# A new order for the first batch of an attention and MLP kernel, and a second weight matrix loaded by rows

## The chip, the cores and the metric

The kernel runs on one core of a Trainium2 chip. The metric is the device time of one execution in microseconds. Before the change the median of three runs is 582.38 us (581.66 to 583.03).

## The reference

Eight batches of 448 tokens, 12 heads of 64 columns. Queries and keys are normalised by rows, attention is computed without a mask, and the result passes a layer norm and an MLP of 768 to 3072 to 768 columns with a residual.

```python
q_n, k_n = (rmsnorm(q, g_q), rmsnorm(k, g_k))
scores = scale * np.matmul(q_n, k_n.transpose(0, 1, 3, 2))
attn = np.exp(scores - np.max(scores, axis=-1, keepdims=True))
attn = attn / (np.sum(attn, axis=-1, keepdims=True) + 1e-09)
x = np.matmul(attn, v)          # heads side by side: (8, 448, 768)
xn = (x - mu) / np.sqrt(var + 1e-06) * g_ln
out = x + np.maximum(xn @ w_ch1, 0.0) @ w_ch2
```

## The kernel before

Work is counted in pairs of heads (48 pairs, six a batch) and in units of one or two pairs, by which q, k and v are loaded and prepared. Batch 0 consists of units 0 to 3: unit 0 holds pair 0, unit 1 pair 1, unit 2 pairs 2 and 3, unit 3 pairs 4 and 5. From batch 1 on every unit has two pairs: unit 4 pairs 6 and 7, and so on. A pass over a unit of one pair has 448 columns, over one of two pairs 896.

All engines run their instructions in the order in which the program gives them out. For the first batch, and the preparation of some units of the second, this order is written out by hand in `ORDER` (L36), which `first_attention` (L490) walks through. The entries are:

- the preparation of unit u (`pieces`, L233). `a` and `c` square k and q (on ScalarE, or on GpSimd for those in `POOL_SQUARE`), `d` and `e` sum the squares (VectorE), `g` (or `gq` and `gk`) takes the inverse root on ScalarE, `i` multiplies k by the gains (GpSimd, or VectorE for units in `DVE_KG`), `j` makes k's high half in 16 bits (GpSimd for units in `POOL_HI`, else ScalarE), `k` the low half (GpSimd for `POOL_LO`, else VectorE), `l` scales q (VectorE), `m` copies it into a second half (GpSimd for `POOL_DUP`, else VectorE), and `z` casts v on GpSimd. `i0` also multiplies the two gains and spreads them over the partitions with a small matmul, `psG`.
- `Kp` and `Qp`: seven transposes on TensorE for pair p, and a copy out of PSUM (VectorE; for pairs in `ACT_Q` the copy of q is on ScalarE). The keys of all pairs go through the bank `tr`; the queries of batch 0 through a bank of the pool of three called `mlp`, those of pair 6 on through `tr`.
- `Sp.i` and `Vp.i`: piece i of 7 of the scores of pair p, with the exponential on ScalarE behind each (two banks in turn), and of the product with v; the last piece, `Vp.6`, is followed by two reciprocals and two multiplications on VectorE (`evac_o`, L464).
- `T`, `A`, `R`, `N`, `X`: the statistics of the layer norm, their joining, its root, the normalised tile and its transposes (`ln_trans`, L682: the first tile through `tr` with two copies on ScalarE, the second through an `mlp` bank, the third through `tr` with a copy on VectorE). `U0` to `U2` are the first three columns of tiles of the MLP (`up_first`, L937), one token tile each, with the activation behind `U2`. `M` takes a few minima and maxima for a check at the end.
- `L` loads a unit (SP's queue), `W` a third of W1 (GpSimd's queue), `G` and `G2` load and scale the norm's gain.
- `Hn` and `Jn`: n matmuls whose result nobody reads. `H` multiplies an identity by itself into the bank `psW`, `J` transposes an identity into `tr`. They lie in TensorE's queue like any other matmul.

Behind the list, `run_rest` (L976) goes through the batches. It takes the MLP of batch b in chunks (`mlp_chunks`), and between them gives out the steps of the attention of batch b+1 (`attention`, L540), spread evenly so that they end `TAIL[b]` chunks ahead of the batch's end; the layer norm of the next batch follows in these last chunks. Batch 0 has 21 chunks of the up projection (`up`, L713) and then 24 of the down projection (`down`, L723): for each of two column halves g and three token tiles t, four chunks of six of the 24 row tiles of W2. A bank of the pool `mlp` collects all 24, and `add` (L754) then adds it into x on VectorE, scaled.

From batch 1 on the down projection uses sums of blocks of W2 (a scheme with seven products in place of eight). With W2 in four blocks B11 to B22 (rows by columns), T1 = B12 - B11, T2 = B22 - T1, T3 = B12 - B22 (in place) and T4 = B21 - T2, each cut into four parts. `weight_sums` (L760) makes them on VectorE, one part behind each of certain chunks: eight parts, T1 and T2 in turn, in the last ten chunks of batch 0, then T3 and T4 in batch 1.

W2 is loaded by GpSimd's queue with a cast (`load_w2`, L611), at the steps `W2_AT` of the attention: its left column half as one transfer, later its right half as two.

Of the kernel before, what the change touches and what calls it, by code (L numbers as in the profile page):

```python
# [8 lines left out]
FP32 = mybir.dt.float32  # L9
# [7 lines left out]
ts = bass.ts  # L17
# [9 lines left out]
EXP_BIAS = -4.0  # L27
DVE_KG, POOL_HI, POOL_DUP, ACT_Q = (0, 6), (1, 2, 3, 4, 5, 6, *range(8, 25)), (3, 4, 5, 6), (0, 2, 4, 5)
POOL_SQUARE, POOL_LO = ((2, 1), (4, 0), (6, 0)), (5, 6)

# [61 lines left out]
class _Fast:  # L92
# [140 lines left out]
    def pieces(self, u):  # L233
# [4 lines left out]
        c = {}  # L238
# [86 lines left out]
        def qdup():  # L325
            (nc.gpsimd if u in POOL_DUP else nc.vector).tensor_copy(out=c["qn"][:, :, 1],
                                                            in_=c["qn"][:, :, 0])

# [34 lines left out]
    def trans_k(self, p):  # L363
        nc, sh = self.nc, self.sh
        u, w = PAIR_UNIT[p]
        qn, khl = self.units[u][0:2]
        kT, ps = self.kU[PE_SET][:, 960 * (p % 2):960 * (p % 2) + 960], self.tr
        nc.tensor.matmul(ps[:, 0:256].rearrange("p (e o) -> p e o", e=2)[:, :, 0:D],
                         khl[:, self.group(p, 6)], sh.id16, is_transpose=True, start=True, stop=False)
        for i in range(6):  # L370
            nc.tensor.matmul(ps[:, 192 + 128 * i:320 + 128 * i], khl[:, self.group(p, i)], sh.id16,
                             is_transpose=True, start=False, stop=(i == 5))
        nc.vector.tensor_copy(out=kT, in_=ps[:, 0:960])

# [236 lines left out]
    def load_w2(self, g):  # L611
        if g:
            self.nc.gpsimd.tensor_copy(out=self.rr[:, DMA_UNIT:DMA_UNIT + 1],
                                       in_=self.kU[DMA_UNIT % 2][:, 0:1])
        for c in (slice(0, HALF), slice(HALF, NFF)) if g else (slice(0, NFF),):
            self.nc.gpsimd.dma_start(
                out=self.sh.w2[:, c, ts(g, 384)],
                in_=self.w2[128 * c.start:128 * c.stop, ts(g, 384)].rearrange("(c p) d -> p c d", p=128))

# [88 lines left out]
    def first_mlp(self):  # L708
# [39 lines left out]

# [11 lines left out]
    def weight_sums(self):  # L760

        nc, w2, w2s = self.nc, self.sh.w2, self.w2s
        sub = lambda out, a, b: nc.vector.tensor_tensor(out=out, in0=a, in1=b, op=ALU.subtract)  # L763
# [212 lines left out]
    def run_rest(self):  # L976
        steps, mark, upto = self.steps, self.mark, self.upto
        for b in range(B):
# [19 lines left out]
            for cost, emit in chunks:  # L998
# [252 lines left out]
```

## Time and profile before

| | |
|---|---|
| median of three runs | 582.38 us |
| the profiled execution's own time | 579.58 us |
| its span in the trace | 578.0 us |
| TensorE busy | 559.5 us, 97% of the span |
| VectorE busy | 381.7 us, 66% |
| ScalarE busy | 364.4 us, 63% |
| GpSimd busy | 207.0 us, 36% |

The span runs from the first to the last instruction of the profiled execution; 1.58 us of its own time lie around it. Times in the timelines count from the span's start. A row of a timeline gives the start, the length, the engine (PE is TensorE, DVE VectorE, ACT ScalarE, POOL GpSimd), the line of the kernel, the operation, its tiles, and in brackets how long the engine had been idle and what it seems to have waited for. A matmul's length holds its way through the array, so that matmuls in a row overlap; how fast they follow each other is read from how much longer a longer row takes.

### The profile page before, as it was taken

Reading aid. Unit: us, or ns where it says so; the run is one execution under the profiler, and the core shown is the slowest. Engines: PE = TensorE matmul, PEld = TensorE weight load, DVE = VectorE, ACT = ScalarE, POOL = GpSimd, SP = SyncE. Lnnn points to the kernel's source line nnn. Section 1 sums busy time; section 2 is a strip of 40 time slices with the busy share of each in tenths; the row PEclk is TensorE's granted clock in tenths of the full one; section 3 lists DMA queues with packets and bytes.
Section 4 is the critical chain, followed back from the end, with each engine's and each line's share of the span. In section 5 each row is a group of like instructions: output and inputs, shape, how many; then the busy total and the mean of one; then the engine's idle time right before and its main releaser. Section 6 shows DMA issues by size and latency. Waiting matters only on the chain.

```text
span 578.0 us, 13670 instructions
## 1 busy us (share of the span) xinstructions
PE 559.5 (97%) x5446; PEld 411.9 (71%) x5446; DVE 381.7 (66%) x826; ACT 364.4 (63%) x674; POOL 207.0 (36%) x224
## 2 busy tenths in 40 slices
PE   5788999999999999999999999999999999999997
PEld 4556666687686867777677768777777777878684
DVE  6989567699657586845667586854756743664424
ACT  5998787447675779557775588637777477323130
POOL 5885636404440620654241521644242320020000
PEclk9999999999999999999999999999999999999999
DMA  8999999958672876969663798958743390030201
GB/s 206 251 238 222 214 207 165 193 147 137 124 131 77 158 127 145 127 148 121 121 106 48 184 134 136 128 143 122 145 64 65 119 113 1 1 110 1 83 2 58
DMA packets 178329, 72.59 MB, mean 126 GB/s; under 512 B 138212, under 2 KB 173220, under 8 KB 178260
## 3 DMA queue, kind: packets, MB, share of 16 engines
q1 hardware_dynamic: 133876, 52.52, 44.1%
q0 software_dynamic: 43440, 18.52, 25.2%
q8 instruction: 44, 0.72, 0.5%
q10 hardware_dynamic: 944, 0.62, 0.4%
q14 instruction: 25, 0.20, 0.1%
HBM read 52.76 MB, written 11.01 MB: 110 GB/s over the span
## 4 chain that ended last, share of the span: by engine, by line
PE 77%; DVE 1%; issue 0%; DVEq 0%
PE psH L798 33%; PE psP L821 30%; PE psS L405 7%; PE oA L458 4%; PE oB L460 1%; PE psS L411 1%; DVE qn L83 0%; DVE w2s L763 0%; DVE ssq L265 0%; DVE w L763 0%; DVE xn L662 0%; DVE hS L804 0%; DVE x L475 0%; DVE xl L757 0%; DVE xl L480 0%
## 5 line engine op out<-in xcount | busy, mean ns | idle before, releaser
L421 ACT ACTIVATE E<-psS,rr_all 128x448 f16<-128x448 f32 x336 | 204.6, 634 | 47.3 <-PE psS L405 40.3
L798 PE MATMUL psH<-xnT,w 128*128 128x256 f16 (+1 forms) x2016 | 225.7, 261 | 0.0
L798 PEld LDWEIGHTS <-w 128*128 128x128 f16 x2016 | 172.8, 98 | 24.3 <-issue 4.9
L801 ACT ACTIVATE hS<-psH 128x512 f16<-128x512 f32 x150 | 89.8, 599 | 97.2 <-PE psH L798 93.0
L821 PEld LDWEIGHTS <-hS 128*128 128x128 f16 x1080 | 100.0, 98 | 57.3 <-issue 1.1
L821 PE MATMUL psP<-w,hS 128*128 128x384 f16 x672 | 127.0, 326 | 0.0
L405 PE MATMUL psS<-qU,kU 128*128 128x448 f16 x288 | 100.9, 352 | 5.0 <-ACT E L421 3.2
L458 PEld LDWEIGHTS <-E 128*128 128x128 f16 x1008 | 70.3, 98 | 35.8 <-issue 2.8
L279 POOL TENSOR_TENSOR k<-k,gprod 128x896 f32<-128x896 f32 x18 | 38.9, 2160 | 139.5 <-ACT khl L259 113.2
L804 DVE TENSOR_TENSOR hS<-hS 128x512 f16<-128x512 f16 (+1 forms) x119 | 60.2, 512 | 19.3 <-ACT hS L801 17.8
L821 PE MATMUL psP<-w2s,hS 128*128 128x384 f16 (+1 forms) x408 | 69.9, 321 | 0.0
L458 PE MATMUL oA<-v,E 128*128 128x65 f16 x864 | 66.9, 193 | 1.1 <-ACT E L421 0.6
L757 DVE SCALAR_TENSOR_TENSOR x<-psP,rs_all,x 128x384 f32<-128x384 f32 x60 | 36.4, 617 | 42.4 <-PE psP L821 41.8
L460 PE MATMUL oB<-v,E 128*128 128x65 f16 x288 | 52.0, 193 | 0.1
L832 POOL TENSOR_TENSOR x<-x,hS 128x384 f32<-128x384 f32 x21 | 23.4, 1126 | 76.1 <-ACT hS L900 75.5
L473 DVE RECIPROCAL rec_all<-oA 128x6 f32<-128x6 f32 x48 | 9.2, 193 | 53.6 <-PE oA L458 53.5
L216 POOL DMA_DIRECT2D v<-in_v_dram x54 | 41.5, 781 | 4.0 <-PE oB L460 2.7
L405 PEld LDWEIGHTS <-kU 128*128 128x128 f16 x288 | 28.0, 98 | 11.1 <-issue 2.2
L900 ACT ACTIVATE hS<-hS,rs_all 128x384 f32<-128x384 f32 x27 | 14.6, 604 | 33.0 <-DVE hS L804 33.0
L460 PEld LDWEIGHTS <-E 128*128 128x128 f16 x336 | 32.4, 96 | 0.4 <-DVE xl L480 0.3
L83 DVE SCALAR_TENSOR_TENSOR qn<-q,rr_all 128x256 f16<-128x256 f32 (+2 forms) x69 | 24.8, 420 | 7.2 <-ACT rr_all L269 7.1
L265 DVE TENSOR_REDUCE ssq<-khl 128x14 f32<-128x896 f32 (+1 forms) x24 | 25.5, 1061 | 5.0 <-ACT khl L259 4.8
(145 smaller groups left out, 616.6 us busy)
## 6 DMA issues: line engine op xcount, KB each, us to landing
k<-in_k_dram SPq DMA_DIRECT2D x19, 384.0 KB, 4.2
q<-in_q_dram SPq DMA_DIRECT2D x18, 384.0 KB, 3.9
out_dram<-x SPq DMA_DIRECT2D x14, 384.0 KB, 3.0
w<-in_moe_w_ch_dram POOLq DMA_DIRECT2D x3, 1536.0 KB, 14.3
v<-in_v_dram POOLq DMA_DIRECT2D x54, 64.0 KB, 4.4
out_dram<-x POOLq DMA_DIRECT2D x9, 384.0 KB, 2.7
w<-in_moe_w_ch_dram POOLq DMA_DIRECT2D x1, 2304.0 KB, 22.5
w<-in_moe_w_ch_dram POOLq DMA_DIRECT2D x2, 1152.0 KB, 14.4
```

Source lines behind the costliest of these rows:

```text
L216: nc.gpsimd.dma_start(out[:, :, j, 0:D], main[:, :, j])
L265: nc.vector.tensor_reduce(out=c["ssq"][:, n], in_=c["sq", n], axis=AX.X, op=ALU.add)
L279: (nc.vector if u in DVE_KG else nc.gpsimd).tensor_tensor(out=c["t"][1], in0=c["t"][1], in1=sh.gprod.unsqueeze(1).broadcast_to([128, g, D] ...
L405: nc.tensor.matmul(ps[0][:, 0:S], c["main"][:, ts(i, 128)], c["q"][:, ts(h, S)], start=True, stop=True)
L421: nc.scalar.activation(out=o, in_=x[:, 0:S], func=AFT.Exp, scale=self.units[u][3][:, g:g + 1], bias=EXP_BIAS)
L458: nc.tensor.matmul(oA[:, t, cs], E[:, ts(t, 128)], rhs, start=(i == 0 and t == 0), stop=(i == 6 and t == 2))
L460: nc.tensor.matmul(oB[:, cs], E[:, 320:448], rhs, start=(i == 0), stop=(i == 6))
L757: self.nc.vector.scalar_tensor_tensor(out=x, in0=ps, scalar=self.rs[:, b, t:t + 1], in1=x, op0=ALU.mult, op1=ALU.add)
L798: nc.tensor.matmul(ps[:, i], sh.w1[:, dc, ts(f + i, 128)], self.xnT[:, dc, 256 - N:256], start=(i == 0 and dc == 0), stop=(i == k - 1 and ...
L801: nc.scalar.activation(out=hT[:, f:f + k], in_=ps, func=AFT.Relu)
L804: nc.vector.tensor_tensor(out=out, in0=a, in1=c, op=op)
L821: nc.tensor.matmul(bank[x][:, c], a[:, f], w[:, f, c], start=(start and f == 0), stop=(stop and f == HALF - 1))
```

## The change

It has four parts.

- `ORDER` is sorted anew. It has the same entries apart from `H` and `J`: 180 matmuls in `H` (76 before) and 23 in `J` (32 before). Some work changes its engine: the squares of k of units 5 and 6 go to GpSimd, that of unit 2 to ScalarE; the high half of unit 2 goes to ScalarE; the low half of unit 4 and the gains of unit 6 go to GpSimd; the doubling of q goes to GpSimd for unit 0 and to VectorE for units 5 and 6; the copies of `Q2` and `Q5` go to VectorE. Two new lists, `ACT_K` and `ACT_DUP`, are empty.
- W2 is loaded by rows: at each of the two steps two transfers of 768 rows and all 768 columns.
- The down projection of batch 0 goes over both column halves and all three token tiles with the first 12 row tiles, then again with the last 12. Each round collects in a bank of its own, so that `add` runs twelve times instead of six. `store_late` moves from `s == 3` to `s == 5`.
- The weight sums are made in the order T1, T3, T2, T4: T1's four parts in the last six chunks of batch 0, the rest in batch 1. `TAIL[0]` is 10 instead of 11.

```diff
-DVE_KG, POOL_HI, POOL_DUP, ACT_Q = (0, 6), (1, 2, 3, 4, 5, 6, *range(8, 25)), (3, 4, 5, 6), (0, 2, 4, 5)
-POOL_SQUARE, POOL_LO = ((2, 1), (4, 0), (6, 0)), (5, 6)
+DVE_KG, POOL_HI, POOL_DUP, ACT_Q = (0,), (1, 3, 4, 5, 6, *range(8, 25)), (0, 3, 4), (0, 4)
+ACT_K, ACT_DUP = (), ()
+POOL_SQUARE, POOL_LO = ((4, 0), (5, 1), (6, 0), (6, 1)), (4, 5, 6)
 ORDER = """
-b0 H12 a0 L4 c0 i0 e0 j0 H24 b1 gq0 d0 k0 l0 a1 m0 K0 G gk0 i1 H10 L5 c1 Q0 d1 j1 S0.0 b2 S0.1
-H5 a2 e1 g1 S0.2 c2 S0.3 k1 l1 z0 d2 e2 m1 K1 S0.4 i2 H16 S0.5 S0.6 Q1 g2 H5 J8 b3 l2 j2 k2 c3
-V0.0 S1.0 z2 S1.1 S1.2 V1.0 J8 a3 m2 H4 V0.1 z3 S1.3 K2 S1.4 V0.2 Q2 V0.3 V0.4 d3 S1.5 V0.5 V0.6
-S2.0 S1.6 V1.1 V1.2 S2.1 e3 W0 i3 K3 V2.0 S2.2 V2.1 S2.3 Q3 j3 T0 S2.4 k3 V1.3 g3 V1.4 S2.5 S2.6
-l3 b4 V1.5 m3 c4 S3.0 S3.1 V2.2 S3.2 K4 a4 V1.6 S3.3 V2.3 S3.4 Q4 d4 V2.4 V2.5 V3.0 V3.1 V3.2
-V2.6 i4 S3.5 j4 J4 S3.6 V3.3 T1 K5 e4 k4 S4.0 W1 S4.1 S4.2 Q5 z4 b5 S4.3 V3.4 V4.0 V3.5 S4.4
-V4.1 V4.2 S4.5 W2 V4.3 S5.0 g4 V3.6 S4.6 S5.1 J4 V5.0 V4.4 G2 S5.2 l4 T3 K6 V4.5 V5.1 V4.6 S5.3
-T4 V5.2 a5 L6 V5.3 S5.4 m4 Q6 i5 S5.5 V5.4 S5.6 V5.5 V5.6 T5 S6.0 S6.1 J4 S6.2 A V6.0 S6.3 V6.1
-N0 N1 S6.4 S6.5 J4 V6.2 X0 V6.3 d5 j5 N2 S6.6 V6.4 X1 z5 Q7 c5 V6.5 R U0 e5 U1 g5 X2 V6.6 M k5
-U2 K7 b6 L7 a6 L8k c6 i6 l5 m5 e6 d6
+H21 L4 b0 a0 H1 H5 c0 i0 H22 e0 d0 j0 H8 H13 gq0 H8 k0 H7 gk0 l0 b1 m0 H8 a1 c1 Q0 d1 G e1 H4 L5
+K0 H8 H13 g1 i1 H8 b2 a2 S0.0 S0.1 H11 j1 c2 l1 k1 H8 S0.2 S0.3 z0 H8 m1 d2 K1 i2 e2 S0.4 S0.5
+g2 S0.6 Q1 V0.0 V0.1 V0.2 H4 j2 H5 l2 S1.0 b3 k2 z3 c3 S1.1 S1.2 H17 H1 z2 a3 S1.3 m2 V1.0 V0.3
+Q2 K2 S1.4 S1.5 V1.1 V0.4 S2.0 d3 V0.5 V0.6 W0 V1.2 S2.1 S1.6 S2.2 e3 S2.3 V1.3 i3 K3 j3 g3 Q3
+l3 b4 m3 c4 S2.4 V2.0 S2.5 S2.6 V1.4 S3.0 V2.1 a4 k3 V1.5 S3.1 T0 V1.6 K4 S3.2 V2.2 d4 S3.3 V3.0
+Q4 V3.1 i4 V2.3 S3.4 T1 V2.4 V2.5 V2.6 e4 V3.2 S4.0 J7 S3.5 S3.6 Q5 S4.1 j4 S4.2 W1 V3.3 k4 V4.0
+K5 S4.3 V4.1 V3.4 S4.4 V3.5 S4.5 b5 W2 z4 V3.6 T3 V4.2 S5.0 V4.3 g4 S5.1 S5.2 V4.4 V5.0 l4 S4.6
+K6 V5.1 G2 S5.3 m4 V4.5 L6 V4.6 S5.4 V5.2 Q6 S5.5 a5 V5.3 S5.6 V5.4 V5.5 T4 V5.6 z5 T5 S6.0 i5
+S6.1 V6.0 S6.2 S6.3 J16 S6.4 A V6.1 V6.2 N0 N1 V6.3 d5 S6.5 j5 X0 c5 N2 Q7 X1 e5 V6.4 S6.6 U0 X2
+L7 k5 U1 K7 L8k M g5 b6 V6.5 R U2 a6 V6.6 l5 c6 d6 m5 i6 e6
 """.split()
...
-TAIL = (11, 13, 17, 13, 17, 13, 19, 0)
+TAIL = (10, 13, 17, 13, 17, 13, 19, 0)
...
-        for c in (slice(0, HALF), slice(HALF, NFF)) if g else (slice(0, NFF),):
+        for c in (0, 6) if not g else (12, 18):
             self.nc.gpsimd.dma_start(
-                out=self.sh.w2[:, c, ts(g, 384)],
-                in_=self.w2[128 * c.start:128 * c.stop, ts(g, 384)].rearrange("(c p) d -> p c d", p=128))
+                out=self.sh.w2[:, c:c + 6],
+                in_=self.w2[128 * c:128 * c + 768].rearrange("(c p) d -> p c d", p=128))
...
         def down(t, g, s):
-            if s == 0:
-                cur["ps"] = self.ps_m.tile([128, 512], FP32, tag="mlp", name="psC")
-            ps = cur["ps"][:, 0:HCOL]
+            if s in (0, 4):
+                cur[t] = self.ps_m.tile([128, 512], FP32, tag="mlp", name="psC")
+            ps = cur[t][:, 0:HCOL]
             for f in range(3 * s, 3 * s + 3):
                 nc.tensor.matmul(ps, hT[:, f, ts(t, 128)], sh.w2[:, f, ts(g, HCOL)],
-                                 start=(f == 0), stop=(f == NFF - 1))
+                                 start=(f % HALF == 0), stop=(f % HALF == HALF - 1))
+            if s in (3, 7):
+                self.add(0, t, g, ps)
             if s == 7:
-                self.add(0, t, g, ps)
...
-            elif s == 3:
+            elif s == 5:
                 self.store_late()
...
-        for g in range(2):
-            for t in range(3):
-                for s in range(4):
-                    yield 6 * HCOL / 2.4, [lambda t=t, g=g, s=s: down(t, g, s)
-                                           for s in (2 * s, 2 * s + 1)]
+        for g, s, t in [(g, s, t) for r in (0, 2) for g in range(2) for t in range(3) for s in (r, r + 1)]:
+            yield 6 * HCOL / 2.4, [lambda t=t, g=g, s=s: down(t, g, s)
+                                   for s in (2 * s, 2 * s + 1)]
...
-        ops, t4s = [], []
+        ops = [], [], []
...
-            ops += [lambda a=a: sub(*a) for a in ((t1, b12, b11), (t2, b22, t1))]
-            t4s.append(lambda a=(t4, b21, t2): sub(*a))
+            for x, a in zip(ops, ((t1, b12, b11), (t2, b22, t1), (t4, b21, t2))):
+                x.append(lambda a=a: sub(*a))
...
-        return ops, last + t4s
+        return ops[0], last + ops[1] + ops[2]
...
-                if (left < 10 if b == 0 else b == 1) and ops:
+                if (left < 6 if b == 0 else b == 1) and ops:
```

More of the change, by code (lines that the diff above doesn't have):

```diff
@@ L325, in qdup @@
         def qdup():
-            (nc.gpsimd if u in POOL_DUP else nc.vector).tensor_copy(out=c["qn"][:, :, 1],
-                                                            in_=c["qn"][:, :, 0])
+            out, x = c["qn"][:, :, 1], c["qn"][:, :, 0]
+            if u in ACT_DUP:
+                nc.scalar.copy(out=out, in_=x)
+            else:
+                (nc.gpsimd if u in POOL_DUP else nc.vector).tensor_copy(out=out, in_=x)
         def vmain():
@@ L372, in trans_k @@
                              is_transpose=True, start=False, stop=(i == 5))
-        nc.vector.tensor_copy(out=kT, in_=ps[:, 0:960])
+        if p in ACT_K:
+            nc.scalar.copy(out=kT, in_=ps[:, 0:960])
+        else:
+            nc.vector.tensor_copy(out=kT, in_=ps[:, 0:960])
     def trans_q(self, p):
```

## Prediction

> **What bounds the kernel now.** I read the slices of the span first, then a table of three stretches, then the timelines of the engines in the first 60 us.
>
> ```profile
> PE   5788999999999999999999999999999999999997
> ```
>
> ```profile
> 6.00:24.00 18.00, 13.33 (x169) 10.39 (x169) 17.01 (x22) 14.39 (x30) 13.43 (x15) 1.00 0.99 259
> 24.00:47.00 23.00, 18.82 (x242) 12.47 (x240) 20.57 (x46) 21.28 (x40) 17.31 (x15) 1.00 1.10 229
> 57.00:80.00 23.00, 22.25 (x189) 13.98 (x188) 14.82 (x23) 19.83 (x41) 15.94 (x16) 1.00 1.13 218
> 80.00:107.00 27.00, 27.00 (x257) 17.53 (x255) 15.95 (x38) 19.47 (x36) 9.07 (x11) 1.00 1.30 184
> ```
>
> The first shows TensorE short of work in its first four slices only (14.5 us each). In the table (busy us of PE, PEld, DVE, ACT, POOL) TensorE is busy all 27 us of 80 to 107; before 47 it is not: there VectorE works 17.0 of 18 and 20.6 of 23, ScalarE 21.3 of the 23. So the kernel is a start, bound by VectorE and ScalarE, and then TensorE without a gap. TensorE's own work behind the list stays as it is; an edit pays or costs what it moves the moment at which TensorE is full, plus any gap it makes later.
>
> **The start.** Timeline of TensorE, then of VectorE and GpSimd:
>
> ```profile
> 2.74 1.46 PE L532 MATMUL psW<-id 128*128 128x128 f16 x12 [2.74 <-POOL id masks.py:199]
> 5.36 0.68 PE L277 MATMUL psG<-gprod,w 1*128 1x64 f32 x2 [1.16 <-DVE gprod L274]
> 5.98 2.74 PE L532 MATMUL psW<-id 128*128 128x128 f16 x24
> 9.29 0.72 PE L532 MATMUL psW<-id 128*128 128x128 f16 x10
> 10.56 0.23 PE L382 MATMUL psQ<-id,qn 128*128 128x128 f16 x1 [0.55 <-DVE qn L326]
> 12.50 0.44 PE L532 MATMUL psW<-id 128*128 128x128 f16 x5
> ```
>
> ```profile
> 9.40 1.11 DVE L326 COPY qn<-qn 128x448 f16<-128x448 f16 x1
> ```
>
> ```profile
> 8.81 1.55 POOL L279 TENSOR_TENSOR w2s<-w2s,gprod 128x448 f32<-128x448 f32 x1 [4.28 <-ACT khl L259]
> ```
>
> Twelve more identity matmuls cost 2.74 - 1.46 = 1.28 us early, 107 ns each; after 8.9 five more cost 0.72 - 0.44 = 0.28, 56 ns each. So the clock doubled between 8.4 and 8.9, some 3.0 to 3.5 us after the run that begins at 5.36.
>
> The change puts 27 identity matmuls ahead of `psG` (12 before) and then 66 (22+8+13+8+7+8) ahead of `Q0`. The 27 end at 2.74 + 27 x 0.107 = 5.63, 0.27 later than `psG` starts now. That is hidden: what follows `psG` waits for a square on ScalarE anyway. `psG` takes its 0.62, so the 66 start at 6.25. TensorE now works without a break from 2.74; with the same 3.0 to 3.5 us the clock is up by about 6.2, and the 66 end at 6.25 + 66 x 0.056 = 9.9. `Q0` also needs `m0`, the copy that moves from VectorE to GpSimd. Half of the 0.93 us that GpSimd needs for 896 columns (row further down) is 0.5, behind `qn` at 9.4: 9.9 to 10.0. **`Q0` at 10.0 instead of 10.56: -0.56.** Both ends: if the clock comes as late as now (8.9), 25 of the 66 are slow, they end at 8.9 + 41 x 0.056 = 11.2, +0.6; if it doesn't come at all, at 6.25 + 66 x 0.107 = 13.3, +2.7. I take 10.0, because the trace's own delay of 3.0 to 3.5 us gives it. [...]
>
> **From `Q0` to unit 3: ScalarE.**
>
> ```profile
> 11.16 0.91 ACT L388 COPY qU<-psQ 128x896 f16<-128x896 f16 x1 [1.64 <-PE psQ L385]
> 12.51 1.16 ACT L421 ACTIVATE E<-psS,rr_all 128x448 f16<-128x448 f32 x2 [0.44 <-PE psS L405]
> 19.03 0.95 ACT L259 ACTIVATE qn<-w2s 128x896 f32<-128x896 f32 x1 [0.96 <-PE psQ L385]
> 20.12 1.71 ACT L421 ACTIVATE E<-psS,rr_all 128x448 f16<-128x448 f32 x3
> ```
>
> ScalarE copies `Q0` 0.6 after its issue. From there to the end of `S1.0` and `c3` it now needs until about 20.7, with waits of 0.44 and 0.96 and some 0.2 in small ones. The change gives it two more passes over 896 columns in this stretch, `a2` and `j2`, both from GpSimd, each 0.85 to 0.95 like `c3`: 1.7 to 1.9. They fill the waits, no more: the same point comes some 10.1 us behind `Q0` in both, at 20.1. The 52 identity matmuls between `Q0` and `S0.2` (4, 29, 19) last 2.9 us at 56 ns, while ScalarE does `Q0`'s copy, `g1` and `a2`: hidden, or 0.2 late. VectorE takes over the copy of `Q2` and waits for `Q2`'s transposes, which stand behind `S1.3` and so behind those exponentials: it comes to `d3` at 23.1 (23.26 now).
>
> **From `d3` on: VectorE, then GpSimd.**
>
> ```profile
> 23.26 1.08 DVE L265 TENSOR_REDUCE ssq<-khl 128x14 f32<-128x896 f32 x1
> 27.80 0.62 DVE L390 COPY qU<-psQ 128x896 f16<-128x896 f16 x1 [0.43 <-PE psQ L385]
> 29.34 1.08 DVE L83 SCALAR_TENSOR_TENSOR qn<-w2s,rr_all 128x896 f16<-128x896 f32 x1
> 31.42 0.66 DVE L373 COPY kU<-tr 128x960 f16<-128x960 f16 x1 [0.99 <-PE tr L371]
> 38.47 1.08 DVE L290 TENSOR_TENSOR khl<-k,khl 128x896 f16<-128x896 f32 x1
> 39.73 0.20 DVE L473 RECIPROCAL rec_all<-oA 128x6 f32<-128x6 f32 x1 [0.18 <-PE oA L458]
> ```
>
> Here VectorE loses `k4` (1.08, to GpSimd). ScalarE without the copy of `Q2` (0.91) runs ahead, and the waits of 0.43, 0.99 and 0.18 for what its exponentials hold up go; VectorE gains the copy of `Q5` (0.62). That is -2.1 up to `V4.6`; if the waits stay, -0.5. But the list now has `l3` ahead of `k3`, so `l3` ends at 29.0 (30.43 now), and the rest hangs on GpSimd's queue:
>
> ```profile
> 30.58 0.93 POOL L326 COPY qn<-qn 128x896 f16<-128x896 f16 x1 [2.91 <-PE oB L460]
> 39.28 2.27 POOL L507 TENSOR_SCALAR gln<-gln 128x768 f32<-128x768 f32 x1
> 42.24 0.93 POOL L326 COPY qn<-qn 128x896 f16<-128x896 f16 x1 [0.69 <-DVE qn L83]
> ```
>
> ```profile
> L290 POOL TENSOR_TENSOR khl<-hS,khl 128x896 f16<-128x896 f32 x1 | 1.9, 1892 | 0.1
> ```
>
> From `m3` to the end of `G2` GpSimd works 41.55 - 30.58 = 10.97 us: ten instructions, two of them the issues of `W1` and `W2`, which count like the rest. `k4` comes in between at 1.89. So `m4` runs from 29.05 + 10.97 + 1.89 = 41.9 to 42.9 (43.17 now), and what it releases is `Q6`:
>
> ```profile
> 43.91 0.22 PE L382 MATMUL tr<-id,qn 128*128 128x128 f16 x1 [0.15 <-DVE kU L373]
> 46.03 0.34 PE L458 MATMUL oA<-vl,E 128*128 128x130 f16 x3 [0.36 <-ACT E L421]
> 48.76 2.03 DVE L662 SCALAR_TENSOR_TENSOR xn<-x,stat,gln 128x384 f16<-128x384 f32 x3
> 50.30 0.86 ACT L702 COPY w2s<-tr 128x384 f16<-128x384 f16 x2
> 51.21 0.22 PE L382 MATMUL tr<-id,qn 128*128 128x128 f16 x1
> 54.92 1.17 PE L945 MATMUL psU<-w2s,w 128*128 128x128 f16 x18 [0.42 <-DVE w2s L706]
> 56.31 0.98 PE L718 MATMUL psH<-w2s,w 128*128 128x384 f16 x5
> ```
>
> `Q6` goes from 43.91 to 43.0. Behind it stand the last exponentials of pair 5 (without the wait of 0.15, and with `a5` off ScalarE), so `V5.6` starts at 45.0 instead of 46.03 and the norm `N0` by as much: **-1.1**. Then the new order costs something. `Q7` stands right behind `X0`, and both write the bank `tr`, so `Q7` waits for ScalarE's two copies (about 1.3 us from `N0`'s end to theirs, as now). And `K7`, ahead of `U2`, waits for VectorE's copy of `X2`. From `N0`'s end VectorE does `N1` (1.0), `d5` (1.0), `N2` (1.0), `Q7`'s copy (0.6), `e5` (1.0) and `X2`'s copy (0.55), 5.2 in all; TensorE, with `X0`'s copies, `Q7`, `X1`, `S6.6`, `U0`, `X2` and `U1`, is done after 5.0. Then come `K7` (0.4), `V6.5` (0.1), `U2` (1.0) and `V6.6` (0.2): TensorE leaves the list 6.9 us behind `N0`, where now it takes 6.45 (56.31 less `N0`'s end, half of the 2.03 behind 48.76 and a little more). **+0.5**. So the list ends 0.6 earlier.
>
> **What else moves.** `Q8` now waits for VectorE:
>
> ```profile
> 63.03 0.22 PE L382 MATMUL tr<-id,qn 128*128 128x128 f16 x1 [0.34 <-DVE kU L373]
> ```
>
> TensorE stands 0.5 us in front of it. VectorE gives `i6` to GpSimd, which frees 1.78 and takes 0.5 to 0.9 for `m5`: **-0.5**. Of the 180 + 23 fillers (76 + 32 before) the other blocks lie where TensorE waits for exponentials; 95 x 0.056 = 5.3 us is their bound from above if none is hidden, and zero from below.
>
> W2 by rows changes no matmul. It adds six of the sums into `x`, and takes four weight sums out of the last chunks of batch 0, to put them among the first of batch 1:
>
> ```profile
> L763 DVE TENSOR_TENSOR w2s<-w,w2s x8: 744/754/757, 113.9 to 134.2; 128x1152 f16<-128x1152 f16 x8
> ```
>
> ```profile
> L757 DVE SCALAR_TENSOR_TENSOR x<-psP,rs_all,x 128x384 f32<-128x384 f32 x60 | 36.4, 617 | 42.4 <-PE psP L821 41.8
> ```
>
> Six times 0.62 is 3.7 us, mostly before 107, where VectorE has 11 of 27 us free. Each takes a bank that comes round after two further half-sums, about 4 us: free. Four times 0.75 leave a VectorE that is full there, and come back 12 us later: -0.2 for a wait at 131, or +0.3 for one behind it; I take -0.2. `TAIL` lets the attention steps end one chunk (1 us) later, and the transposes of batch 1 with them, which TensorE needs at the end of batch 0: 0 if they have that much to spare, at most +1. I take 0, since VectorE, whose norms they wait for, has four weight sums fewer there. SP's queue keeps the order of its loads (`L4`, `G`, `L5` to `L8k`); the stores of batch 0 go out later and hold nothing. The load:
>
> ```profile
> L616 POOL DMA_DIRECT2D w<-in_moe_w_ch_dram x3: 1032/1063/1507, 61.4 to 88.6; - x3
> DMA to landing us min/median/max: 10.9/17.8/22.5
> ```
>
> The last part, issued at 88.6, lands at 106.4 if it still takes 17.8; it is needed from chunk 14, at 107.6, where now it is chunk 15. Zero, with 1.2 us to spare.
>
> **The sum.** -1.1 + 0.5 - 0.5 - 0.2 = -1.3 us against the profiled execution, 579.58. That one lies 2.8 below the median of the runs, 582.38, and I lay the same difference on the median: **581.1**.
>
> **The rivals.**
> - **The clock comes as late as now.** Everything up to `N0` hangs on `Q0`, so +1.2 for 11.2: the sum is -0.1, 582.3. For it: the trace shows no release before 8.4. Against it: there TensorE had been idle from 4.2 to 5.4.
> - **The fillers stand in the way (slower).** If the clock isn't up within the block of 66, they end at 13.3 and `Q0` is 3.3 later than in my sum: +2.0, 584.4. It beats the gain once the block ends after 11.3, and costs over 0.2% after 12.5. Blocks of 29 and 19 behind it add to this in the same way.
>
> ```profile
> 21.55 0.39 PE L532 MATMUL psW<-id 128*128 128x128 f16 x4
> ```
>
> - **A larger gain.** The timed runs are 2.1 to 3.5 us above the profiled one. If that is a clock that in them rises later or falls back between 9 and 15 us, where TensorE now has 15 fillers, the change (some 60 there) would end it: -2.8, 579.6. The profile can't show it, since it is one execution. [...]
> - **The change of W2 doesn't do what it should.** If the last part took 22.5 like the longest, it would land at 111.1, 3.5 us late: +2.2, 584.6.
>
> **How the numbers follow.** Forecast -1.3 (-2.0 to -0.6) 0.36; late clock 0.19; fillers in the way 0.22; larger gain 0.20; late W2 0.03. What a measurement of this kernel can tell from no change is about 0.2%, 1.2 us. Of the forecast 0.25 lies beyond it and 0.11 within: faster 0.45, within 0.30, slower 0.25. The range leaves out what of the slower cases lies beyond 584.0 and of the larger gain below 578.9, about 0.2 together; the forecast's own is 580.4 to 581.8.
>
> **What would show it.** Identity matmuls of 56 ns from about 6.2 on; `Q0` at 10.0; `m4` ending at 42.9; `Q7` waiting for ScalarE behind `X0`; TensorE leaving the list at 55.7; no wait ahead of `Q8`; none between 84 and 140. It is wrong if slow matmuls last beyond 8.9, if `S0.2` waits behind fillers while ScalarE is idle, or if TensorE waits in the down chunks of batch 0.

## The result, and the profile after

The changed kernel takes 585.38 us (median of 7 runs, 583.73 to 587.91), the kernel before, run beside it, 582.38 (7 runs, 581.66 to 583.18): a ratio of 1.0051 (1.0028 to 1.0075), some 3.0 us slower. Forecast were 581.1 us and a range from 578.9 to 584.0.

The marks of the two profiled executions, from their timelines (us from the span's start):

| | before | after | forecast |
|---|---|---|---|
| `Q0` starts | 10.56 | 10.32 | 10.0 |
| `m4` ends on GpSimd | 43.17 | 44.39 | 42.9 |
| `Q6` starts | 43.91 | 44.45 | 43.0 |
| `V5.6` starts | 46.03 | 46.45 | 45.0 |
| the list ends (first `up` behind `U2`) | 56.31 | 57.27 | 55.7 |
| batch 1's first `up` | 118.36 | 119.19 | 117.3 |
| last matmul starts | 573.9 | 576.0 | 572.6 |
| span; own time | 578.0; 579.58 | 582.1; 583.73 | |

The forecasts of the last rows are those of the list and of the sum, laid on before's. TensorE's row of the slices of after:

```profile
PE   7878999999999999999999999999999999999995
```

The first two slices are fuller (fillers), the third goes from 8 to 7 and holds the idle place found below, the rest looks like before's: a loss of 3 in 580 us hardly shows in forty slices. It is found by the same marks in both timelines.

**`Q0` came nearly as forecast, but its lead was gone at once.** TensorE's timeline of after, then VectorE's copy of `K0` and ScalarE's first exponentials:

```profile
2.75 3.06 PE L539 MATMUL psW<-id 128*128 128x128 f16 x27 [2.75 <-POOL id masks.py:199]
6.00 0.43 PE L278 MATMUL psG<-gprod,w 1*128 1x64 f32 x2 [0.19 <-DVE gprod L275]
6.36 3.86 PE L539 MATMUL psW<-id 128*128 128x128 f16 x66
10.32 0.23 PE L389 MATMUL psQ<-id,qn 128*128 128x128 f16 x1
...
11.33 1.78 PE L539 MATMUL psW<-id 128*128 128x128 f16 x29
12.95 0.54 PE L412 MATMUL psS<-qU,kU 128*128 128x448 f16 x2
```

```profile
11.53 0.66 DVE L380 COPY kU<-tr 128x960 f16<-128x960 f16 x1 [0.83 <-PE tr L375]
```

```profile
13.34 1.16 ACT L428 ACTIVATE E<-psS,rr_all 128x448 f16<-128x448 f32 x2 [0.32 <-PE psS L412]
```

The 66 take 3.86 us, nearly all of them 56 ns; the trace's records of the granted clock have it full from 5.86 (8.63 before). But `S0.0`, whose operands are both there at 12.19, stands behind the 29 fillers until 12.95 (12.12 before), and ScalarE is idle for 0.32 us because of it. The point forecast at 20.1, the end of `S1.0` and `c3`, is at 20.71, where before had it, and `d3` starts at 23.40 (23.1 forecast, 23.26 before).

**The list then falls behind on GpSimd.** GpSimd's timeline, VectorE's rows for `k3` and `l4`, and what TensorE waits for:

```profile
29.25 1.66 POOL L331 COPY qn<-qn 128x896 f16<-128x896 f16 x1 [1.79 <-DVE qn L84]
...
36.45 1.90 POOL L291 TENSOR_TENSOR khl<-k,khl 128x896 f16<-128x896 f32 x1
...
40.67 2.84 POOL L514 TENSOR_SCALAR gln<-gln 128x768 f32<-128x768 f32 x1
43.47 0.92 POOL L331 COPY qn<-qn 128x896 f16<-128x896 f16 x1
```

```profile
29.03 1.08 DVE L291 TENSOR_TENSOR khl<-w2s,khl 128x896 f16<-128x896 f32 x1
...
40.32 1.19 DVE L84 SCALAR_TENSOR_TENSOR qn<-hS,rr_all 128x896 f16<-128x896 f32 x1
```

```profile
44.45 0.23 PE L389 MATMUL tr<-id,qn 128*128 128x128 f16 x1 [2.53 <-POOL qn L331]
...
51.86 0.22 PE L389 MATMUL tr<-id,qn 128*128 128x128 f16 x1 [0.95 <-ACT w2s L709]
...
57.27 0.49 PE L725 MATMUL psH<-w2s,w 128*128 128x384 f16 x2
```

`m3` takes 1.66 us where it took 0.93; it now begins 0.2 behind the start of `k3` on VectorE and ends 0.80 behind its end. `G2` takes 2.84 where it took 2.27; it begins 0.35 behind the start of `l4` and ends 2.0 behind its end. `m4` and with it `Q6` are 1.5 late against the forecast, and TensorE stands idle for 2.5 us in one piece.

**And TensorE waits in batch 1.** Waits of TensorE from 139 to 146 us, a row of busy times of after and the same of before, and VectorE's timeline with the weight sums:

```profile
PE oA L465 <- DVE x L482: 0.5, 1, 0.5
PE psH L804 <- DVE x L763: 0.4, 1, 0.4
```

```profile
120.00:144.00 24.00, 23.39 (x233) 18.34 (x231) 23.70 (x40) 17.02 (x33) 7.03 (x7) 1.00 0.77 158
120.00:144.00 24.00, 23.95 (x244) 18.99 (x242) 23.23 (x43) 18.02 (x35) 7.01 (x7) 1.00 0.72 135
```

```profile
137.58 2.17 DVE L769 TENSOR_TENSOR w2s<-w,w2s 128x1152 f16<-128x1152 f16 x3
139.68 1.07 DVE L291 TENSOR_TENSOR khl<-k,khl 128x896 f16<-128x896 f32 x1
140.69 1.07 DVE L266 TENSOR_REDUCE ssq<-qn 128x14 f32<-128x896 f32 x1
141.68 0.18 DVE L480 RECIPROCAL rec_all<-oA 128x6 f32<-128x6 f32 x1
```

VectorE is busy 23.70 of 24 us (23.23 before). Three parts of T4 in a row stand ahead of a low half, a sum and then the copy of a finished pair out of PSUM (141.68), whose matmuls had ended at 139.2. By the starts of TensorE's matmuls the three gaps are 0.69, 0.24 and 0.55, 1.5 us; before had one of 0.21 at 131. Batch 1 begins 0.83 later than before, the last matmul 2.1: the 1.27 between are this.

The two spans differ by 4.1, of which 2.0 lie behind the last matmul. SyncE's last rows, before and after:

```profile
573.65 1.47 SPq L959 DMA_DIRECT2D out_dram<-xl  x2
```

```profile
575.75 2.82 SPq L965 DMA_DIRECT2D out_dram<-xl  x2
```

From the start of the last matmul to the span's end before's profile has 4.12 us, after's 6.07, and the twelve further kernels below 5.2 to 6.0, those with before's list too. So this part belongs to the profiled execution of before and not to the change.

### The profile page after: what moved, and what is told of

It reads as the page before. It is cut to its first block, busy times and chain, and to the rows that moved or that the text cites. A ratio compares the mean times of both kernels' runs of the same rounds, so it can differ in the third digit from the quotient of the medians.

```text
span 582.1 us, 13855 instructions
## 1 busy us (share of the span) xinstructions
PE 563.0 (97%) x5541; PEld 416.6 (72%) x5541; DVE 381.9 (66%) x833; ACT 363.4 (62%) x672; POOL 210.5 (36%) x226
## 3 DMA queue, kind: packets, MB, share of 16 engines
q1 hardware_dynamic: 133876, 52.52, 42.9%
## 4 chain that ended last, share of the span: by engine, by line
PE 74%; DVE 3%; issue 0%
PE psH L804 32%; PE psP L827 29%; PE psS L412 6%; PE oA L465 4%; PE oB L467 1%; PE psS L418 1%; DVE w2s L769 1%; DVE hS L810 0%; DVE ssq L266 0%; DVE x L763 0%; DVE qn L84 0%; DVE x L482 0%; DVE khl L291 0%; DVE w L769 0%; DVE xl L487 0%
## 5 line engine op out<-in xcount | busy, mean ns | idle before, releaser
L280 POOL TENSOR_TENSOR k<-k,gprod 128x896 f32<-128x896 f32 x19 | 41.5, 2183 | 140.2 <-ACT khl L260 97.6
```

The source lines that it names most:

```text
L280: (nc.vector if u in DVE_KG else nc.gpsimd).tensor_tensor(out=c["t"][1], in0=c["t"][1], in1=sh.gprod.unsqueeze(1).broadcast_to([128, g, D] ...
```

## The experiments

Each of four groups ran on one chip together with the kernel before (e1 to e4, e5 to e8, e9 and e10, e11 and e12); there before's median is 581.83, 581.58, 581.60 and 581.48 us. "List", "b1" and "last" are the marks above; "clock" is when the trace has the granted clock full first.

| | median us (range; runs) | ratio (95%) | clock | list | b1 | last |
|---|---|---|---|---|---|---|
| e1 list alone | 584.07 (581.68 to 587.18; 12) | 1.0037 (1.0018 to 1.0056) | 6.00 | 57.24 | 118.78 | 574.4 |
| e2 W2 and sums alone | 582.66 (581.94 to 583.64; 12) | 1.0012 (1.0000 to 1.0023) | 9.52 | 56.87 | 118.43 | 575.5 |
| e3 old order of sums | 586.70 (584.23 to 588.05; 6) | 1.0070 (1.0049 to 1.0091) | 7.77 | 58.99 | 121.88 | 578.9 |
| e4 `G2` behind `m4` | 584.56 (582.30 to 585.58; 12) | 1.0036 (1.0022 to 1.0050) | 8.74 | 58.70 | 120.62 | 577.4 |
| e5 matmul filler | 583.59 (582.42 to 583.93; 7) | 1.0034 (1.0019 to 1.0048) | 6.75 | 57.49 | 119.71 | 576.2 |
| e6 transpose filler | 583.37 (581.92 to 585.95; 8) | 1.0035 (1.0017 to 1.0053) | 8.68 | 58.09 | 119.14 | 576.0 |
| e7 `m4` moved, sums later | 581.75 (581.11 to 583.93; 12) | 1.0012 (1.0000 to 1.0023) | 7.83 | 56.82 | 118.74 | 574.5 |
| e8 old list, sums later | 581.71 (580.75 to 582.34; 12) | 1.0000 (0.9990 to 1.0010) | 9.12 | 56.93 | 118.49 | 574.2 |
| e9 list mended further | 582.08 (581.15 to 582.69; 11) | 1.0009 (0.9996 to 1.0021) | 8.56 | 57.53 | 119.45 | 575.2 |
| e10 no early fillers | 583.62 (582.87 to 584.95; 7) | 1.0034 (1.0022 to 1.0046) | 15.75 | 59.34 | 121.26 | 577.0 |
| e11 before, more fillers | 581.21 (580.76 to 583.22; 12) | 0.9996 (0.9982 to 1.0010) | 10.83 | 56.41 | 118.46 | 574.7 |
| e12 e8, more fillers | 581.26 (580.46 to 582.05; 12) | 0.9999 (0.9986 to 1.0012) | 12.20 | 56.50 | 118.05 | 573.7 |

**e1 and e2: each half alone.** e1 is the change with before's `load_w2`, `first_mlp`, `weight_sums`, `TAIL` and `left < 10`; e2 is the kernel before with the change's.

> The changed kernel with the load of W2, the down projection of batch 0, the weight sums and TAIL as before; only the list and its engine tables are new. Theory (GpSimd's queue holds Q6 up in the list, and the weight sums hold batch 1 up later, two separate costs): TensorE leaves the list 1.0 us later than before (57.3), has no wait over 0.3 us between 138 and 146, and its last matmul starts 0.8 later than before, near 574.7. Rival (the list costs nothing in the end, all comes from the MLP part): last matmul within 0.3 of 573.9. Second rival (180 identity matmuls make the clock or the start worse, the MLP part nothing): the whole 2 us at the last matmul stay.

> The kernel before with only the load of W2 by rows, the two rounds, the new order of the weight sums and TAIL 10; the list as before. Theory: the list ends at 56.3 as before; TensorE waits 1.3 to 1.5 us near 141 for VectorE, which has four weight sums more there; the last matmul starts 1.2 to 1.3 later than before, near 575.2. Rival: the wait near 141 comes from the list, whose delay stays in VectorE's queue; then there is none here and the last matmul is within 0.3 of before.

The two ratios add up to the change's: 1.0037 and 1.0012. The list is slower; e2's interval begins at 1.0000, and what it loses is read from its trace: e2 has the gaps of 0.70, 0.24 and 0.55 at 141 to 144, e1 none there. e1's executions scatter over 5.5 us, e2's over 1.7. Each of e1's twelve lists its mean granted clock: the four at 0.998 to 1.000 have spans of 580.1 to 581.4 us, the four at 0.993 to 0.994 583.7 to 585.6. So the list costs little in some executions and 4 us in others. The mean clock alone doesn't prove the cause (it also holds the half clock at the program's end, 0 to 3.8 us in the fourteen profiles, and before at 0.994 has 580.9 and 581.9), so what has to be found are half-clock stretches inside the span.

**e3: the weight sums as before, in the changed kernel.**

```diff
-                if (left < 6 if b == 0 else b == 1) and ops:
+                if (left < 10 if b == 0 else b == 1) and ops:
```

and T1 and T2 in turn, then T3 and T4, as before.

> The changed kernel with the weight sums in the order of before (T1 and T2 in turn in the last ten chunks of batch 0, then T3 and T4); W2 by rows and the two rounds stay. Theory: the wait near 141 goes, the last matmul starts 1.2 to 1.5 earlier than in the changed kernel (576.0), near 574.7. Rival: the six added sums into x fill VectorE at the end of batch 0, so that with T2 back there TensorE waits for a bank between 112 and 119 or for T3 near 131; gain under 0.5.

No gain: TensorE waits at 118.9 for a bank that `add` has not emptied (0.85) and at 134.7 for the copy of a pair (0.90 and 0.22). Waits of TensorE from 115 to 137:

```profile
PE oA L465 <- DVE x L482: 0.7, 1, 0.7
PE psC L735 <- DVE x L763: 0.7, 1, 0.7
```

With six more `add` in batch 0, T2's parts have no free place at its end either. The median can't be read as the price of the order alone, since this profile, and e4's, hold such a stretch.

**e4: `G2` behind `m4`.**

```diff
-K6 V5.1 G2 S5.3 m4 V4.5 L6
+K6 V5.1 S5.3 m4 G2 V4.5 L6
```

> The changed kernel with the scaling of the gain (G2, 2.3 to 2.8 us on GpSimd) behind m4 instead of ahead of it. Theory: m4 starts when l4 ends (41.5) and not at 43.5, Q6 starts near 42.6 instead of 44.45, TensorE leaves the list 1.5 to 1.9 earlier, near 55.6, and the last matmul starts as much earlier, near 574.3. Rival (VectorE or ScalarE would hold Q6 up anyway, or the fillers do): Q6 moves by under 0.5 and the last matmul by under 0.5.

GpSimd's timeline of e4:

```profile
42.48 0.93 POOL L331 COPY qn<-qn 128x896 f16<-128x896 f16 x1 [1.07 <-DVE qn L84]
43.39 2.15 POOL L514 TENSOR_SCALAR gln<-gln 128x768 f32<-128x768 f32 x1
```

`m4` is 1.0 earlier though this clock rose 2.9 us later, and `G2` takes 2.15, with copies out of PSUM and the steps of a pair beside it on VectorE, but not `l4`. `Q6` (43.46) and `Q7` (50.82) are 1.0 ahead of the change's. Yet the list ends at 58.70, not at the 55.6 expected: `X1` waits 0.77 for `N1`, and `U0`, `X2` and most of `U1` run at half clock. Busy times by stretches of 3.413 us, the length of the half-clock stretch in both traces, counted from the rise of the clock (columns: length, PE, PEld, DVE, ACT, POOL, then PEclk); first e3, then e4:

```profile
41.90:45.31 3.41, 0.58 (x11) 0.37 (x9) 1.69 (x5) 0.95 (x2) 3.31 (x4) 1.00 1.13 215
45.31:48.73 3.42, 3.13 (x27) 2.11 (x25) 1.50 (x5) 1.27 (x2) 3.28 (x5) 0.50 1.11 226
```

```profile
49.70:53.12 3.42, 1.56 (x23) 1.17 (x22) 3.42 (x3) 2.35 (x5) 1.57 (x1) 1.00 1.13 207
53.12:56.53 3.41, 3.41 (x36) 3.41 (x34) 3.06 (x4) 1.66 (x6) 3.24 (x2) 0.50 1.11 227
```

**In these two profiles the clock goes back to half for exactly one such stretch** (0.50, 1.00 behind it), behind one in which TensorE was busy 0.58 (e3) and 1.56 (e4) of 3.41 us; no gap in either was over 3.0 us, and in the second none over 1.1. A stretch at half clock that is busy throughout loses at most half of its 3.413 us, 1.7, an estimate. In the profile of the change itself nothing of the kind is seen; its stretches cut the weak place in two:

```profile
39.99:43.40 3.41, 1.93 (x27) 1.41 (x26) 3.29 (x8) 2.31 (x4) 3.25 (x3) 1.00 1.13 215
43.40:46.82 3.42, 2.04 (x27) 1.50 (x28) 1.32 (x5) 1.16 (x2) 3.42 (x5) 1.00 1.11 222
41.10:44.51 3.41, 0.88 (x15) 0.65 (x14) 2.19 (x6) 1.30 (x3) 3.41 (x3) 1.00 1.13 213
```

A stretch that begins at 41.10 would hold 0.88. The same place of before:

```profile
41.10:44.51 3.41, 2.62 (x39) 1.90 (x37) 3.31 (x8) 2.99 (x5) 1.75 (x3) 1.00 1.13 212
```

**e5 and e6: a filler in the idle place.** 24 identity matmuls (e5, a new entry `I`) or identity transposes (e6, `J24`) into the bank `tr`, ahead of `Q6`.

```diff
-V5.2 Q6 S5.5
+V5.2 I24 Q6 S5.5
```

> The changed kernel with 24 identity matmuls (into the bank tr, which the copy behind K6 has left by then) in TensorE's idle place ahead of Q6; all else as in the change. The idle place is 2.7 us long in the changed kernel's profile, so the 24 (24 x 55 ns = 1.3 us) should delay nothing. Theory: much of the loss is the granted clock, which goes back to half for a window of 3.4 us when the window before it held too little work on TensorE; in the changed list the weakest 3.4 us hold 18% of matmul time (from 41 us on), in the list before never under 43% behind 15 us, and the profiles with a half window had 12% and 39% ahead of it. With the filler the weakest window holds about 50%, so the half windows should all but go: mean granted clocks of 0.997 to 1.0 in most runs, spread as narrow as before's (2 us), and a median 1.5 to 2.3 us better than the change's, 1.001 to 1.0025 of the time before. What is left over 1 is the list's own lateness (0.4 us at batch 1's start) and the wait at 141 us (1.3). Rival: the clock has nothing to do with that place, or has its price elsewhere: ratio 1.004 to 1.006 as with the change, clocks of 0.99 to 0.998.

> The same with 24 identity transposes in place of the 24 matmuls, into the same bank at the same place; they should take the same 1.3 us. If any work on TensorE holds the clock, this one gives what the one with the matmuls gives (1.001 to 1.0025). [...]

e5's timeline shows that the filler delays nothing (`Q6` still waits for `m4`):

```profile
42.47 1.50 PE L542 MATMUL tr<-id 128*128 128x128 f16 x24 [0.33 <-DVE kU L380]
44.66 0.23 PE L389 MATMUL tr<-id,qn 128*128 128x128 f16 x1 [0.70 <-POOL qn L331]
```

e5's seven executions lie within 1.5 us (the change's within 4.2), all at clocks of 0.998 to 1.000 (the change's at 0.990 to 0.998), and the median is 1.8 below the change's, as expected; but the change was not run again beside it, and the two ratios' intervals overlap. My figure for the ratio was too low, since what remains (0.8 at batch 1's start, 1.3 at 141) is 1.0036 by itself.

e5's profile also shows W2 late for once: its last part, issued at 91.70 and not at 89.31 as in the change's profile, landed at 107.81, and the seventh matmul of the second round, the first that needs it, comes 0.56 late:

```profile
107.85 0.65 PE L739 MATMUL psC<-w,hS 128*128 128x384 f16 x3 [0.39 <-DMA q<-in_q_dram]
```

(The profile names another load that ended last.) So 0.56 of the lateness of e5's batch 1 is not the list's.

e6 gives the same median; six of its eight executions have 0.999 or 1.000, one, at 0.996, is at 585.95. e6's stretches:

```profile
42.81:46.22 3.41, 2.46 (x38) 2.10 (x38) 1.69 (x6) 0.64 (x2) 3.41 (x3) 1.00 1.13 218
46.22:49.63 3.41, 2.44 (x27) 1.32 (x26) 2.81 (x12) 2.56 (x5) 3.27 (x5) 1.00 1.11 223
```

```profile
43.06 1.50 PE L542 MATMUL tr<-id 128*128 128x128 f16 x24 [0.33 <-DVE kU L380]
45.26 0.23 PE L389 MATMUL tr<-id,qn 128*128 128x128 f16 x1 [0.70 <-POOL qn L331]
45.33 0.50 PE L392 MATMUL tr<-id,qn 128*128 128x128 f16 x6
```

Of the 2.46 us in the first, about 2.0 are transposes, and the clock stays full behind it (1.00 from 46.22 to 49.63), in the one execution that shows it. In before's profile, too, the four identity matmuls at 21.55, right behind eight transposes, take 0.39 us, as long as the change's four at 10.72, where the record has the clock full.

**e7: both places mended.** `m4` on VectorE ahead of `K6`'s copy, T4's parts from the twentieth chunk of batch 1 on.

```diff
-... (0, 3, 4), (0, 4)
+... (0, 3), (0, 4)
-K6 V5.1 G2 S5.3 m4 V4.5 L6
+m4 K6 V5.1 G2 S5.3 V4.5 L6
-                if (left < 6 if b == 0 else b == 1) and ops:
+                if (left < 6 if b == 0 else b == 1 and (len(ops) > 4 or left <= late_sums)) and ops:
```

(`late_sums` is the batch's number of chunks less 20.)

> The change with its two suspected places mended and no filler: m4 on VectorE, ahead of K6's copy, and not behind G2 on GpSimd; and T4's four weight sums not among the first sixteen chunks of batch 1's MLP (131 to 139 us in the profile) but from the twentieth on (some 150 us, T4's first product at 156). Theory: Q6 starts at 42.7 to 43.3 (44.45 in the change), so the weakest window of 3.4 us is near 45% and the half windows become rare; the list ends at 55.6 to 56.4 at the same phase of the clock; the wait of 1.5 us at 141 to 144 is under 0.4; last matmul 573 to 574.5, median 581.0 to 582.5, ratio 0.9985 to 1.001. Rival for m4: 0.3 to 1.0 us of m4 on VectorE make K6's copy and V4.6's steps that much later, so that N0 and the list's end stay where the change has them (57.3). Rival for the sums: the four go to another full stretch and the wait appears ahead of T4's product at 156, so the median stays over 583.

The time is in the range that the theory gave, the ratio a little above it. `Q6` now waits for `K6`'s copy, not for `m4`, 43.59, a little later than expected, and the list ends at 56.82. Waits of TensorE from 139 to 158:

```profile
PE psP L827 <- DVE w2s L769: 0.2, 1, 0.2
```

The gaps at 141 to 144 are gone; one of 0.36 ahead of T4's product at 156 is what is left of 1.5. But batch 1 still begins 0.4 later than before.

**e8: the sums' shift with the old list.** The same `late_sums` in e2.

> The list of before with the change's W2, rounds and weight sums, and T4's four sums from the twentieth chunk of batch 1 on. Without the shift this gave a ratio of 1.0012 and waits of 0.70, 0.24 and 0.55 at 141 to 143.5. Theory: the waits are VectorE's backlog of sums and go (to 0.2 to 0.4 in all), worth 1.1 to 1.3 us: 581.3 to 581.7, ratio 0.9985 to 0.9995, since batch 1 starts 0.5 us nearer to the list's end than before. Rival: the wait is the batch's rounds of adds and not the sums, or returns at 150 to 158: ratio 1.0005 to 1.002.

Compared with e2 the last matmul comes 1.3 earlier, and the ratio goes from 1.0012 to 1.0000, just above what the theory gave. So T4's place is the loss of the MLP half, and the rest of that half (W2 by rows, the two rounds, the new order) gains nothing that can be measured. e7 has the same MLP half, so its 1.0012 is what the mended list still costs, if anything: the two intervals touch.

**e9: two more late places of the list mended**, on top of e7: `m5` on GpSimd ahead of `i6`, and `V6.4 S6.6 X1` ahead of `Q7`.

> The version with m4 on VectorE and T4's sums later, and two more of the list's late places mended: m5 on GpSimd ahead of i6 (there it was 1.27 us on VectorE, beside i6's 2.9 us on GpSimd, with Q8 waiting 0.87 for it), and V6.4, S6.6 and X1 ahead of Q7, which waited 1.1 us for X0's copies. Theory (the list is late because of GpSimd's and VectorE's chains at its end): Q8's wait is 0 to 0.3, Q7's under 0.5, the list ends at 55.9 to 56.5 at the same phase of the clock, batch 1 starts at 117.2 to 118.0, last matmul 573.0 to 573.8; median 580.2 to 581.2 where before is 581.6, ratio 0.997 to 0.9995. Rival: what is saved at Q7 and Q8 is waited for at the next place (K7's bank, the first batch's W2 or a copy of VectorE's), batch 1 starts at 118.5 or later and the ratio is 1.000 to 1.002.

The rival came true. `Q7`'s wait becomes one of 1.2 ahead of `X0` and one of 1.0 in `U0`; and `Q8` still waits 0.87, but for another: VectorE's timeline has

```profile
62.78 1.09 DVE L266 TENSOR_REDUCE ssq<-qn 128x14 f32<-128x896 f32 x1 [1.67 <-POOL qn L258]
63.90 0.66 DVE L380 COPY kU<-tr 128x960 f16<-128x960 f16 x1
```

`K8`'s copy stands behind the sum of `e6`, and that waits for a square on GpSimd, which `m5` has pushed back. Mending one place by another queue moved the wait.

**e10: e7 without the 93 identity matmuls ahead of `Q0`.**

> The version with m4 on VectorE and T4's sums later, without the 93 identity matmuls ahead of Q0 (those behind stay). Theory: the fillers bring the full clock earlier (at 5.9 to 8.7 us here, 8.6 to 9.5 with the old list), and without them the full clock comes at 10 to 13 us and Q0 to K1 run at half: each of Q0's, K0's and S0's passes takes twice its time, and the list ends 0.3 to 1.0 us later, ratio 1.002 to 1.003 against 1.0012 with them. Rival: TensorE waits for VectorE's and ScalarE's first units there, so that the clock's start is worth nothing: ratio 1.0005 to 1.0015, or better, since Q0 no longer stands behind a filler (H8 ahead of it ended 0.3 us after Q0's data).

```profile
10.43 0.29 PE L389 MATMUL psQ<-id,qn 128*128 128x128 f16 x1 [3.95 <-POOL qn L331]
...
12.33 3.30 PE L539 MATMUL psW<-id 128*128 128x128 f16 x29
15.42 0.71 PE L412 MATMUL psS<-qU,kU 128*128 128x448 f16 x2
```

`Q0` is not late, but the clock is full only at 15.75, and the 29 fillers that the list keeps ahead of `S0.0` take 3.30 us, mostly ahead of that (1.78 in the change, where the clock is full by then). The list ends 2.5 later than e7's, the median is 1.9 higher, both more than the theory gave. The later fillers were this cheap only with the early ones ahead of them.

**e11 and e12: more fillers in the old list** (23 for 12 at the head, 8 more behind `Q0`), in the kernel before and in e8.

> The kernel before with 19 more identity matmuls and nothing else: 23 for 12 at its head, where TensorE is idle from 4.1 to 5.4 us, and 8 behind Q0, where it is idle from 11.4 to 12.1. Theory (an earlier clock is worth 0.2 to 0.3 us for each us, by the version without the early fillers, whose clock rose 7.9 us later and whose list ended 2.5 us later): the rise comes at 5.9 to 8.7 us and not at 8.6 to 9.5, the list ends 0.2 to 0.6 us earlier, ratio 0.9985 to 0.9998. Rival: the old list's TensorE waits there for other engines, so the clock is worth nothing and the ratio is 0.9995 to 1.0005, or above if a filler delays Q0 or S0.0.

> The same 19 identity matmuls in the version with the old list, the change's W2 and weight sums, and T4's sums later, which gave 1.000 without them. Theory: the 0.2 to 0.6 us of the earlier clock come off whole, ratio 0.9985 to 0.9998; this would be the best version here. Rival: nothing is gained, 0.9995 to 1.001.

Neither differs measurably from before. The rise did not come earlier in these two profiles (10.83 and 12.20, 8.63 in before's), and the old list ends at 56.4 to 56.5 all the same (56.31 before); so its end hardly moved with the rise. What the rise needs stays open: in e11 TensorE was busy 3.27 us of the 3.42 from 4.00 to 7.42, and the clock stayed at half, while the change's rise followed a stretch (2.45 to 5.86) with 3.06. No version here beats the kernel before.

## Why the prediction was wrong

- **`Q0` at 10.0: right where the rise came early.** 10.32 in the profile of the change, where the rise was at 5.86. In e4 and e9, with the same fillers, it was at 8.74 and 8.56, and `Q0` at 11.17 and 11.09. The first matmuls start at 2.75 in all three, so the rise came 3.1, 6.0 and 5.8 us behind them, and the 3.0 to 3.5 that I took from before's trace were no fixed delay. By the trace's record full clock lasted 573.44 us in the change's profile and 570.03 in before's, 168 and 167 times 3.413 us, which is also their difference; what sets the moment of the rise no run shows. The rises at 5.86 and 6.00 (e1) lie ahead of the 6.2, and no rise followed e11's busy stretch. Of eight profiles with these fillers three had `Q0` at 10.3, two at 10.7 and three at 11.1 to 11.2: the rival of the late clock is as common as the case that I forecast.
- **The fillers behind `Q0`, "hidden, or 0.2 late": mis-sized.** ScalarE lost 0.32 to the 29 ahead of `S0.0`, and `d3` came 0.3 later than forecast. The sizes fit; no run takes out these 29 alone, so their price at the list's end isn't shown. With the late clock fillers hold up `Q0` too: in e6 (rise at 8.68) `m0` ended at 10.15, and `Q0` started at 11.15. (The 95 matmuls of the prediction's bound are not in the other blocks: these hold 58, before 57.)
- **VectorE's stretch from `d3` to `V4.6`: right in the main.** `d3` at 23.40 for 23.1; `V4.6`'s steps end at 43.42, 1.66 ahead of before's (2.1 or 0.5 forecast).
- **`m4` at 41.9 to 42.9: the step that failed first.** I added GpSimd's ten durations as before had them and put `k4` in at its own price. 0.2 came from a later start of `m3`, 0.73 from `m3` beside `k3` and 0.57 from `G2` beside `l4`: 1.5 in all. In e4, where neither stands beside them, `m4`, a copy like `m3`, takes 0.93 and `G2` 2.15, although VectorE works there too; e4's own `m3`, again beside `k3`, takes 1.66. So in these profiles the long times go with `k3` and `l4` beside them, and not with any work of VectorE; why is not shown. `V5.6` came 0.42 later, not 1.1 earlier.
- **The tail of the list, +0.5: right.** 0.96 at its end less 0.42 is 0.54, with `Q7` behind `X0`'s copies as described.
- **`Q8`, -0.5: wrong.** The gap grew from 0.50 to 0.87. `i6`'s 1.78 left VectorE, but ahead of `K8`'s copy came `m5` at 1.27 (0.5 to 0.9 forecast), `l5` at 1.67 for 1.08, and the four steps behind `V6.6` (57.42 to 58.73), which before had ahead of the list's end. With `m5` gone the copy waits for `e6` instead (e9). Between the list's end and batch 1 the change gained 0.13 in all.
- **W2's load and the twelve `add`: right about batch 0.** No gap of 0.2 us between 84 and 140 in the change's profile. The last part landed at 106.16, 1.2 ahead of its use at 107.33, as forecast; e5 shows how little that is. Among the four loads the slowest took 19.0:

```profile
DMA to landing us min/median/max: 10.3/14.7/19.0
```

- **The weight sums, -0.2 or +0.3: the second step that failed.** +1.3, as e2 against e8 shows. I looked at the places which the sums left and not at a VectorE that was already busy 23.23 of the 24 us from 120 to 144 before, to which the new order adds.
- **The clock as a price.** Behind the start I had it among the rivals only as a gain. The list leaves TensorE idle for 2.5 us beside other weak stretches, and behind a weak stretch of 3.413 us (0.58 us of work in e3, 1.56 in e4) the next was at half clock. No profile of the change itself caught one, but the mean clocks of its executions show them: 0.990 to 0.993 over 584.5 to 586.4 us is 8 to 12 us at half clock in three of the seven, where the profiles' ends hold at most 3.8. That they lie at such places is inferred from e3 and e4 and from the spread that e5's filler takes away.

The sum: of the forecast's terms -1.1 became +0.42, +0.5 stayed, -0.5 became -0.13 and -0.2 became +1.27, 2.1 at the last matmul of the profile where -1.3 was forecast. The other 0.9 of the 3.0 I put down to the half-clock stretches in the longer executions; it fits e5's 1.0034 against 1.0051, and those intervals leave it open. The rival of the fillers in the way ended at 584.4, near to what was measured, but by luck: it had them at half clock and 3.3 us, and they cost ScalarE 0.32.

## What to carry to other kernels

When work is moved to GpSimd, look at which instruction of VectorE each one will begin beside, and price the whole queue with the durations seen in such places (here 1.7 and 2.8 us for 0.9 and 2.2), since it is VectorE's new order that decides who runs beside whom. Before work goes into a stretch, read that stretch's own busy row: here, at 97% busy, what was shifted there was waited for, 1.5 us. And a wait of TensorE that is hidden by nothing can cost twice, once as itself and once as a half clock behind it (3.413 us in e3 and in e4). Fillers in such a place were free here when they ended before the awaited data came: the 24 ahead of `Q6` did, by 0.70 us, the 29 ahead of `S0.0` did not, and ScalarE lost 0.32.

## What the runs showed of the hardware

- The clock was at half for 3.413 us once in e3's profile and once in e4's, behind stretches that were not idle: TensorE busy 0.58 and 1.56 of 3.41 us. Behind stretches with 1.93 and 2.04 (the change) it stayed full, and so it did behind one with 1.75 (e1, from 40.14).
- The first full clock came between 5.86 and 8.74 in eight profiles with the same fillers ahead of `Q0`.
- In the change's profile two instructions of GpSimd that began beside one of VectorE ended late: the copy of 0.93 us took 1.66, ending 0.80 behind the end of `k3`; the scaling of 2.15 took 2.84, ending 2.0 behind the end of `l4`. Behind the end of `l4` (e4) such a copy took 0.93 and the scaling 2.15.
- The end of the program, from the last matmul on, took 4.12 us in one profile and 5.2 to 6.1 in the thirteen others.
